# One fused kernel on one core: the order planned with a port shared by VectorE and GpSimd, the softmax sum taken from a column of ones, x kept in float32, and four plain d_ff tiles in place of two

## The chip, the core and the metric

The kernel runs on one core of a Trainium2 chip. The metric is the device time of one execution in microseconds. Five engines matter here: TensorE (PE; PEld is its weight load), VectorE (DVE), ScalarE (ACT), GpSimd (POOL), and SyncE (SP), which issues the DMAs. Each engine works through its own queue in order and waits for the others by semaphores.

## The reference

Three stages follow one another, on 2304 tokens (4 batches of 576) and 512 features.

```python
# 1. attention inside chunks of 64 tokens, 8 heads of 64
scores = q_c @ k_c.T / sqrt(64); scores -= max(scores)
attn = exp(scores); attn /= sum(attn) + 1e-9
x = attn @ v_c                      # (2304, 512) after the heads are put side by side
# 2. gated feed-forward, d_ff = 1536
xn = x / sqrt(mean(x*x) + 1e-6) * rms_g
g = xn @ w_gate; val = xn @ w_val
y = (g * sigmoid(g) * val) @ w_out
# 3. four dense experts of width 1024, weighted by p
p = probs / (sum(probs) + 1e-9)
out = sum_e p[:, e] * (relu(y @ w1[e]) @ w2[e])
```

All inputs and the output are float32, except that the program reads w_gate, w_val and w_out as the 32-bit words of a 64-bit layout and puts the float values together itself.

## The kernel before

**Precision.** A matmul operand in float32 is split into a high part (`xh`, `w[:, 0]`, rounded to fp32r by a copy on ScalarE) and a low part (the rest, a subtraction on VectorE or GpSimd). Each product is three matmuls: high by high, high by low, low by high.

**Attention.** Tokens go in 18 tiles of 128. For a tile, SyncE loads q, k and v (line 380); TensorE transposes q and k (415) and makes the scores (445); VectorE takes the maximum (464) and subtracts it (469); ScalarE takes the exponent (482); VectorE sums the exponents (487), adds 1e-9 (488) and inverts (489); GpSimd multiplies the exponents by the inverse (500; VectorE once); TensorE transposes them (511) and multiplies by v (539); the result is copied out of PSUM (552 or 554) and squared and summed on ScalarE (563); GpSimd takes the root (570, 574); VectorE scales by it and by `rms_g` (580); TensorE transposes the row (591, tile `xtps`); ScalarE writes `xh` (599) and VectorE `xl` (604). Tiles 8 to 17 go in pairs up to the division. PSUM banks for all of this are six buffers of one resource, `a`.

**The gated stage.** Tokens are taken in blocks of 512, 512, 512, 512 and 256, and d_ff in 12 tiles of 128. The first `PLAIN` d_ff tiles (two) are plain products (`proj`, matmuls on line 864, PSUM tiles `gps` and `vps`): 12 matmuls for each d_ff tile, block and matrix. The remaining d_ff tiles go in pairs through a seven-product scheme (`seven_first` and `chain`, line 1021, tile `hps`): for two token blocks and two d_ff tiles it needs seven products of six matmuls where plain work needs eight. The last block of 256 is plain throughout (line 1145). The scheme needs sums of x blocks (`first_operands`): four additions that put `xh + xl` together again (960), four sums (965), four low parts (976), each over 1024 elements a partition, for each of two block pairs. The weights need sums too (`block_weights`: line 774, low parts 800).

**Weights of the gated stage.** `converted` turns 64-bit words into float32: one ScalarE step (652), four on VectorE (656, 660, 664, 668) and an addition (674, VectorE or GpSimd). `weights64` splits a plain tile (692, 698). w_out has 12 such tiles; the products with it are `sum_out` (line 1200, tile `yo`). The gated values are stored to DRAM and loaded again (`hidden`, high part 1165, low part 1169).

**The experts.** Two passes over the experts, the block pair (0, 1) and then (2, 3) with the block of 256: `seven` (line 1021), `plain` (1145), `out_product` (1444, gathered by VectorE on 1467).

**What sets the order.** Nothing is written in order by hand. Class `Plan` (lines 18 to 120) holds a list of steps, each with an engine (or two to choose from), an assumed cost, the steps it needs, the buffers it takes and a rank. It places them one after the other at the earliest time that its own costs give, ranks deciding between equals, and emits them in that order. So every engine's queue has a fixed order, and on the chip only semaphores hold an engine back. Plain products of the gated stage are chained through `last_pe` (line 835), so that they keep the order of the list of units.

## Time and profile before

| | |
|---|---|
| three runs, median | 1285.47 us (1285.41 to 1286.49) |
| the profiled execution | 1285.23 us, of which 1283.4 us lie between its first and its last instruction |
| busy share | PE 98%, PEld 82%, DVE 57%, ACT 39%, POOL 26% |
| busy us | DVE 737.9, ACT 505.7, POOL 336.8 |
| DMA | 101 MB, 79 GB/s over the span, 194 and 195 GB/s in its first two fortieths |

Times are counted from the first instruction of the profiled execution. Matmuls are pipelined, so the busy time of one (0.39 us for 512 columns) is longer than the distance to the next; where the text needs the pace of TensorE it takes the distance from start to start. In rows of the timeline the bracket gives how long the engine stood idle before the instruction, and what released it.

### The profile page before, as it was taken

The numbers are of one execution on the slowest core, as the hardware profiler recorded it, in microseconds if no ns is written. First come the engines' busy times: TensorE is split into PE (matmuls) and PEld (weight loads), VectorE is DVE, ScalarE is ACT, GpSimd is POOL, SyncE is SP. The second block draws the span as 40 slices with busy tenths as digits, with TensorE's granted clock in tenths as the row PEclk, the third lists the DMA queues.
The fourth block names the chain that finished last, engine by engine and source line by source line (L and its number), as shares of the span: only waits on it lengthen the run. The fifth ranks groups of instructions, "written<-read, shape, count | busy, mean of one in ns | idle before, by whom it ended". The sixth has DMA issues, their size and how long they took to land.

```text
span 1283.4 us, 17596 instructions
## 1 busy us (share of the span) xinstructions
PE 1252.3 (98%) x6959; PEld 1051.5 (82%) x6959; DVE 737.9 (57%) x1079; ACT 505.7 (39%) x895; POOL 336.8 (26%) x289
## 2 busy tenths in 40 slices
PE   7989799999999999999999999999999999999998
PEld 6777688888888888988888888878888888888887
DVE  5998985677598262644554445484445344454532
ACT  4767344353454242633333324344233233332320
POOL 2576741132033000221211212143132132231200
PEclk9989999999999999999999999999999999999999
DMA  9862132333266331211211112121111111111102
GB/s 194 195 148 76 54 120 77 113 107 108 82 215 201 126 99 50 76 65 33 66 50 52 48 49 67 50 94 54 34 49 34 33 50 36 48 46 37 34 1 82
DMA packets 118674, 101.05 MB, mean 79 GB/s; under 512 B 62400, under 2 KB 94144, under 8 KB 118592
## 3 DMA queue, kind: packets, MB, share of 16 engines
q1 hardware_dynamic: 118592, 99.93, 25.9%
q8 instruction: 54, 0.88, 0.3%
q14 instruction: 28, 0.23, 0.1%
HBM read 81.04 MB, written 18.87 MB: 78 GB/s over the span
## 4 chain that ended last, share of the span: by engine, by line
PE 66%; DVE 1%; issue 0%; ACT 0%
PE y L1444 30%; PE hps L1021 24%; PE yo L1200 9%; PE hps L1145 4%; DVE acc L1293 0%; DVE xa L1306 0%; DVE acc L1467 0%; ACT xa L1300 0%; DVE w L698 0%; ACT w L692 0%; PE hps L1048 0%; ACT hb L1368 0%
## 5 line engine op out<-in xcount | busy, mean ns | idle before, releaser
L1444 PE MATMUL y<-w,hb 128*128 128x512 f32 x1728 | 400.0, 390 | 1.8 <-DVE acc L1467 1.8
L1444 PEld LDWEIGHTS y<-w,hb 128*128 128x128 f32 x1728 | 324.8, 188 | 70.0 <-DVE acc L1467 2.9
L1021 PE MATMUL hps<-xa,w 128*128 128x512 f32 x1344 | 310.4, 390 | 0.0
L1021 PEld LDWEIGHTS hps<-xa,w 128*128 128x128 f32 x1344 | 251.6, 188 | 53.8 <-DVE p L1055 1.9
L1467 DVE SCALAR_TENSOR_TENSOR acc<-y,pn,acc 128x512 f32<-128x512 f32 x126 | 87.6, 748 | 148.3 <-PE y L1444 148.3
L1035 ACT ACTIVATE hps<-hps 128x512 f32<-128x512 f32 x104 | 60.6, 582 | 241.1 <-PE hps L1021 241.0
L1200 PE MATMUL yo<-ha,w 128*128 128x512 f32 (+1 forms) x720 | 148.4, 368 | 0.1
L1200 PEld LDWEIGHTS yo<-ha,w 128*128 128x128 f32 x720 | 125.5, 189 | 23.1 <-DVE w L698 0.5
L800 POOL TENSOR_TENSOR w<-raw,w 128x512 fp32r<-128x512 f32 (+1 forms) x59 | 80.8, 1380 | 211.4 <-ACT w L792 202.8
L733 POOL TENSOR_TENSOR w<-raw,w 128x512 fp32r<-128x512 f32 x39 | 52.7, 1351 | 236.4 <-ACT w L727 235.7
L792 ACT ACTIVATE w<-raw 128x512 fp32r<-128x512 f32 (+1 forms) x128 | 75.4, 601 | 95.9 <-PE y L1444 59.1
L1021 PE MATMUL hps<-xh,w 128*128 128x512 f32 x320 | 105.9, 391 | 0.5 <-ACT hps L1035 0.4
L1052 DVE TENSOR_TENSOR hps<-hps,p 128x512 f32<-128x512 f32 x52 | 36.3, 698 | 120.8 <-ACT hps L1035 120.8
L1021 PE MATMUL hps<-xs,w 128*128 128x512 f32 x360 | 88.5, 390 | 0.3 <-DVE p L1055 0.3
L774 POOL TENSOR_TENSOR raw<-raw 128x256 f32<-128x256 f32 x46 | 37.0, 805 | 191.4 <-DVE w L800 127.4
L1021 PEld LDWEIGHTS hps<-xs,w 128*128 128x128 f32 x360 | 67.3, 188 | 15.2 <-DVE p L1055 1.3
L1169 DVE TENSOR_TENSOR ha<-sr,ha 128x512 fp32r<-128x512 f32 (+1 forms) x60 | 43.5, 750 | 62.6 <-ACT ha L1165 62.6
L1145 PE MATMUL hps<-xh,w 128*128 128x256 f32 x416 | 76.9, 283 | 0.0
L1372 DVE SCALAR_TENSOR_TENSOR hb<-hps,hb 128x512 fp32r<-128x512 f32 x96 | 65.7, 685 | 16.0 <-ACT hb L1368 14.1
L800 DVE TENSOR_TENSOR w<-raw,w 128x512 fp32r<-128x512 f32 (+1 forms) x69 | 46.3, 672 | 46.5 <-ACT w L792 45.5
L1021 PEld LDWEIGHTS hps<-xh,w 128*128 128x128 f32 x320 | 60.3, 188 | 13.8 <-ACT hps L1035 0.8
L1145 PEld LDWEIGHTS hps<-xh,w 128*128 128x128 f32 x416 | 65.7, 192 | 0.5
(115 smaller groups left out, 1547.3 us busy)
## 6 DMA issues: line engine op xcount, KB each, us to landing
raw<-in_moe_w_dram SPq DMA_DIRECT2D x64, 512.0 KB, 3.5
sr<-sd SPq DMA_DIRECT2D x48, 256.0 KB, 3.1
sd<-s SPq DMA_DIRECT2D x38, 256.0 KB, 2.1
raw<-in_moe_w_gate_dram SPq DMA_DIRECT2D x12, 512.0 KB, 4.2
raw<-in_moe_w_val_dram SPq DMA_DIRECT2D x12, 512.0 KB, 3.6
raw<-in_moe_w_out_dram SPq DMA_DIRECT2D x12, 512.0 KB, 3.6
out_dram<-acc SPq DMA_DIRECT2D x18, 256.0 KB, 2.1
q<-in_q_dram SPq DMA_DIRECT2D x16, 256.0 KB, 4.5
```

The source lines that it names most:

```text
L733: e_.tensor_tensor(out=w[:, 1], in0=part(k), in1=f32(w[:, 0]), op=ALU.subtract)
L774: e_.tensor_tensor(out=block(to), in0=block(one), in1=block(two), op=ALU.subtract)
L792: nc.scalar.activation(out=w1t[key, c][:, ms, 0], in_=a, func=AF.Copy)
L800: e_.tensor_tensor(out=w[:, ms, 1], in0=a, in1=f32(w[:, ms, 0]), op=ALU.subtract)
L1021: nc.tensor.matmul(out=bank[b], lhsT=w[:, m, wi, kk, :], rhs=xx[xi][:, kk, :], start=start and (kk, i) == (0, 0), stop=(kk, i) == (1, 2), ...
L1035: nc.scalar.activation(out=bank[to], in_=bank[frm], func=AF.Copy)
L1145: nc.tensor.matmul(out=got["b"], lhsT=w[:, i, wi, kk, :], rhs=(xh, xl)[xi][REST][:, 2 * m + kk, 0:n], start=(m, kk, k) == (0, 0, 0), stop= ...
L1169: nc.vector.tensor_tensor(out=t[:, i, 1], in0=tiles["sd", j, f], in1=f32(t[:, i, 0]), op=ALU.subtract)
L1200: nc.tensor.matmul(out=y_ps[j, d], lhsT=w[:, wi, d, :], rhs=h[:, hl, :], start=first and p == 0, stop=last and p == 2,)
L1372: nc.vector.scalar_tensor_tensor(out=t[:, i, 1], in0=source(), scalar=0.0, in1=f32(t[:, i, 0]), op0=ALU.max, op1=ALU.subtract)
L1444: nc.tensor.matmul(out=y_ps[j, t], lhsT=h[hl][:, t * P:(t + 1) * P], rhs=w[:, wi].rearrange("p k f -> p (k f)"), start=first and (hl, wi) ...
L1467: nc.vector.scalar_tensor_tensor(out=a, in0=ps, scalar=pc, in1=a, op0=ALU.mult, op1=ALU.add)
```

## The change

- **The planner.** A step can now claim a port. Steps that may run on GpSimd claim it, and VectorE steps that read two SBUF operands or make SBUF-to-SBUF passes are marked so by hand. The planner lets a step with the mark begin only when the last one before it has ended, on either engine. This is a rule for the order alone: no semaphore follows from it.
- **Softmax.** v is loaded into tiles of 66 floats a head, whose last two are set to one at the start. The product with v has 65 columns, the last being the sum of the exponents. The division moves behind the product: VectorE adds 1e-9 to the sums in PSUM, inverts them and multiplies the product on its way out of PSUM. The sum over the exponents, the division on GpSimd and the copy out of PSUM go. The product takes a PSUM tile of two banks (`av`); the resource `a` keeps four.
- **x in float32.** ScalarE copies each transposed tile once more, into `xf`; the sums of `first_operands` read `xf`, and the eight additions of `xh + xl` go.
- **Plain tiles.** `PLAIN` is 4: d_ff tiles 0 and 1 for all five blocks, then 2 and 3 for all five. The steps of a plain product are no longer chained to the other products.
- **Buffers and costs.** The places of the sums, of the weight tiles and some assumed costs change; `STRETCH` goes from 1.6 to 1.3.

```diff
-    def add(self, eng, cost, emit, needs=(), takes=(), rank=0.0, lag=0.0, table=None, after=0.0):
+    def add(self, eng, cost, emit, needs=(), takes=(), rank=0.0, lag=0.0, table=None, after=0.0, port=None):
...
+        n.port = len(n.engs) > 1 and "Pool" in n.engs or eng == "Pool" if port is None else port
...
-        t = max(self.free_at.get(eng, 0.0), n.at)
+        t = max(self.free_at.get(eng, 0.0), n.at, self.port_free if n.port else 0.0)
...
+            if n.port:
+                self.port_free = s + cost
...
-    PLAIN = 2
+    PLAIN = 4
...
-    plan.buffers("a", ["a0", "a1"] + [f"y{d}" for d in range(KD)])
+    plan.buffers("a", [f"y{d}" for d in range(KD)])
+    plan.buffers("av", ["av"])
...
-        plan.buffers("w", [f"x{i}" for i in range(4, NWX)], at)
+        plan.buffers("w", ["x8"], at)
...
-    for j, fs in [(0, [0]), (1, [0]), (0, [1]), (1, [1])] + [(j, range(PLAIN)) for j in range(2, NB)]:
-        for f in fs:
-            units += [("g", ("g", f), j), ("v", ("v", f), j)]
+    for f0 in range(0, PLAIN, 2):
+        for j in range(NB):
+            for f in (f0, f0 + 1):
+                units += [("g", ("g", f), j), ("v", ("v", f), j)]
...
-        def total(_):
-            ee = tiles["ee", key]
-            den = sm_p.tile([P, ng * H, 1], F32, tag="den", name="den")
-            nc.vector.tensor_reduce(out=den, in_=ee, axis=AX.X, op=ALU.add)
-            nc.vector.tensor_scalar(out=den, in0=den, scalar1=1e-9, scalar2=None, op0=ALU.add)
-            nc.vector.reciprocal(out=den, in_=den)
...
-            dv = add({"Pool": 1.1, "DVE": 0.69} if i < 2 else "Pool", 1.1, divide, needs=[tot], rank=rank(i, 11))
...
-            s3 = add("PE", 0.436, transpose_e, needs=[dv] + s3s, takes=["a", "eT"], rank=rank(i, 10))
+            s3 = add("PE", 0.436, transpose_e, needs=[ex] + s3s, takes=["a", "eT"], rank=rank(i, 10))
...
-                ps = a_bank(tag, [P, H, D], "xps")
+                ps = ps_a.tile([P, 2, 512], F32, tag=tag, name="xps")
+                ps = ps[:, :, 0:HP * VW].rearrange("p b (h e) -> p b h e", e=VW)
...
+            def total(_, i=i):
+                den = sm_p.tile([P, 2, HP, 1], F32, tag="den", name="den")
+                ps = tiles["xps", i]
+                nc.vector.tensor_scalar(out=den, in0=ps[:, :, :, D:D + 1], scalar1=1e-9, scalar2=None, op0=ALU.add)
+                nc.vector.reciprocal(out=den, in_=den)
+                tiles["den", i] = den
...
+                nc.vector.tensor_tensor(
+                    out=xs.rearrange("p (b h d) -> p b h d", b=2, h=HP), in0=tiles.pop(("xps", i))[:, :, :, 0:D],
+                    in1=tiles.pop(("den", i)).to_broadcast([P, 2, HP, D]), op=ALU.mult,
+                )
...
-            cx = add({"ACT": 0.6, "DVE": 0.69}, 0, copy_x, needs=[s4], rank=rank(i, 7))
-            cx.gives.append(("a", s4, 0))
+            tot = add("DVE", 0.4, total, needs=[s4], rank=rank(i, 7.5))
+            cx = add("DVE", 0.66, divide, needs=[tot], rank=rank(i, 7))
+            cx.gives.append(("av", s4, 0))
...
-            sl = add("DVE", 0.9, scale, needs=[ro, g_node], rank=rank(i, 4))
+            sl = add("DVE", 0.7, scale, needs=[ro, g_node], rank=rank(i, 4), port=True)
...
+            def keep(_, i=i):
+                j, t = tile_block[i]
+                if j not in xf:
+                    xf[j] = big.tile([P, KD, blocks[j][1]], F32, tag=f"acc{j}", name="xf")
+                nc.scalar.activation(out=xf[j][:, :, t * P:(t + 1) * P], in_=tiles["xtps", i], func=AF.Copy)
...
-        for fn, cost in ((c2, 0.5), (c3, 0.88), (c6, 0.5), (c7, 0.75)):
-            n = add("DVE", cost, fn, needs=[n], rank=rank)
-        n = add({"DVE": 0.83, "Pool": 1.45}, 0, c8, needs=[n], rank=rank)
+        for fn, cost in ((c2, 0.43), (c3, 0.69), (c6, 0.43), (c7, 0.69)):
+            n = add("DVE", cost, fn, needs=[n], rank=rank, port=True)
+        n = add({"DVE": 0.69, "Pool": 1.4}, 0, c8, needs=[n], rank=rank)
...
-            node = pe(cost, emit, [w_node[key], *x_nodes[j]] if kk == 0 else [], ["h"] if kk == 0 else [], due[u])
+            node = add("PE", cost, emit, needs=[node] if kk else [w_node[key], *x_nodes[j]],
+                       takes=[] if kk else ["h"], rank=due[u])
...
-        t1 = whole("A21")
-        t2 = whole("A22")
-        s1 = sum_of("A22", "A21", "A22", ALU.add, t1, t2)
...
+        s1 = sum_of("S1", "A21", "A22", ALU.add, *needs)
+        s3 = sum_of("S3", "A11", "A21", ALU.subtract, s1)
+        s2 = sum_of("S2", "S1", "A11", ALU.subtract, s3)
...
+        for i in range(3):
+            t = v_tiles[f"v_{i}"] = at_p.tile([P, H, VW], F32, tag=f"v_{i}", name="v")
+            nc.gpsimd.memset(t[:, :, D:VW], 1.0)
```

Three places show what this does to the queues. First VectorE in the middle of the attention, around a scaling by the root (580 before, 584 now). Before:

```order
L580 SCALAR_TENSOR_TENSOR xs<-xs,rinv,g_bc 128x512
L660 SCALAR_TENSOR_TENSOR f64a<-f64a,raw 128x4x128
L487 TENSOR_REDUCE den<-e 128x16
L488 TENSOR_SCALAR den<-den 128x16
L489 RECIPROCAL den<-den 128x16
L464 TENSOR_REDUCE mx<-sc 128x8
L604 TENSOR_TENSOR xl_99<-xtps,xh_94 128x4x128
```

Now, from the first instruction of the first weight tile (673) on:

```order
L673 TENSOR_SCALAR raw<-f64a 128x512
L548 TENSOR_SCALAR den<-xps 128x8
L549 RECIPROCAL den<-den 128x8
L554 TENSOR_TENSOR xs<-xps,den 128x512
L677 SCALAR_TENSOR_TENSOR f64a<-f64a,raw 128x4x128
L681 TENSOR_SCALAR raw<-f64a 128x512
L685 SCALAR_TENSOR_TENSOR raw<-raw 128x512
L584 SCALAR_TENSOR_TENSOR xs<-xs,rinv,g_bc 128x512
L691 TENSOR_TENSOR f64a<-f64a,raw 128x4x128
```

The sum over the exponents (487) is gone from VectorE, and the inverse stands directly ahead of the division out of PSUM (554), for one tile at a time. The first weight tile (673 here, 656 before) stands behind seven scalings now, and behind three before.

Second TensorE where the plain products of the last block end; `xh_93` is the high part of x of block 0, `xh_97` that of block 4. Before, the seven products begin (1048, 1021):

```order
L864 MATMUL vps<-xl_102,w 128x256
L864 MATMUL vps<-xh_97,w 128x256
L1048 MATMUL hps<-xh_93,w 128x512 x2
L1021 MATMUL hps<-xh_93,w 128x512
L1021 MATMUL hps<-xl_98,w 128x512
```

Now the plain products of d_ff tiles 2 and 3 begin, again with block 0:

```order
L880 MATMUL vps<-xl_102,w 128x256
L880 MATMUL vps<-xh_97,w 128x256
L880 MATMUL gps<-xh_93,w 128x512
L880 MATMUL gps<-xl_98,w 128x512
L880 MATMUL gps<-xh_93,w 128x512 x2
```

A second round of plain products for all blocks stands between the last transposed tile of x and the first seven products.

Third VectorE in the conversion of w_out. Before (656 to 668 convert, 1169 is the low part of a gated tile, 698 that of a weight tile):

```order
L656 TENSOR_SCALAR raw<-f64a 128x512
L660 SCALAR_TENSOR_TENSOR f64a<-f64a,raw 128x4x128
L664 TENSOR_SCALAR raw<-f64a 128x512
L668 SCALAR_TENSOR_TENSOR raw<-raw 128x512
L1169 TENSOR_TENSOR ha<-sr,ha 128x512 x2
L698 TENSOR_TENSOR w<-f64a,w 128x512
```

Now (673 to 685 convert, 691 is the addition, 1180 and 715 the low parts):

```order
L673 TENSOR_SCALAR raw<-f64a 128x512
L677 SCALAR_TENSOR_TENSOR f64a<-f64a,raw 128x4x128
L715 TENSOR_TENSOR w<-f64a,w 128x512
L681 TENSOR_SCALAR raw<-f64a 128x512
L685 SCALAR_TENSOR_TENSOR raw<-raw 128x512
L1180 TENSOR_TENSOR ha<-sr,ha 128x512
L691 TENSOR_TENSOR f64a<-f64a,raw 128x4x128
```

The addition (691) and more of the low parts (715) stand on VectorE now. Over the twelve tiles of w_out VectorE has 8 additions and 10 low parts of weights where it had 3 and 5; GpSimd has 4 and 2 where it had 9 and 7.

## Rows read from the trace of the kernel before

**Rows 1.** The page's first line.

```profile
span 1283.4 us, 17596 instructions
```

**Rows 2.** Busy us by stretch: PE, PEld, DVE, ACT, POOL (instructions), PE clock, DMA share, GB/s.

```profile
0.00:37.10 37.10, 30.18 (x493) 27.03 (x495) 22.67 (x43) 19.62 (x38) 8.59 (x18) 0.95 0.95 199
37.10:135.80 98.70, 88.44 (x1118) 73.36 (x1112) 94.58 (x128) 66.53 (x115) 69.16 (x62) 0.97 0.55 130
135.80:160.30 24.50, 17.25 (x95) 15.42 (x96) 23.63 (x22) 7.13 (x12) 18.68 (x9) 0.89 0.14 46
160.30:345.80 185.50, 185.09 (x903) 156.50 (x903) 125.03 (x188) 81.86 (x145) 46.47 (x41) 1.00 0.31 102
345.80:413.60 67.80, 67.30 (x317) 55.54 (x315) 64.10 (x89) 32.72 (x58) 23.40 (x16) 1.00 0.57 187
```

**Rows 3.** Chain of waits, in order of time: start, length, engine, tile, line, count.

```profile
412.88 0.70 DVE w L698
...
562.45 9.52 PE hps L1021 x42
571.97 10.88 PE y L1444 x48
...
863.33 5.75 PE hps L1145 x48
```

**Rows 4.** Timeline of TensorE: start, length, engine, line, operation, count, idle before.

```profile
4.86 0.60 PE L415 MATMUL tps<-ident,q 128*128 128x128 f32 x4
...
24.18 1.15 PE L445 MATMUL sc<-kT,qT 64*64 64x64 f32 x32
25.25 0.66 PE L415 MATMUL tps<-ident,q 128*128 128x128 f32 x4
25.75 0.60 PE L415 MATMUL tps<-ident,k 128*128 128x128 f32 x4
26.18 0.60 PE L591 MATMUL xtps<-ident,xs 128*128 128x128 f32 x4
...
55.22 0.47 PE L864 MATMUL gps<-xh,w 128*128 128x512 f32 x1
...
135.98 0.63 PE L591 MATMUL xtps<-ident,xs 128*128 128x128 f32 x4 [1.00 <-DVE xs L580]
...
160.27 1.05 PE L1048 MATMUL hps<-xh,w 128*128 128x512 f32 x2
```

**Rows 5.** Timeline of VectorE.

```profile
35.65 0.20 DVE L489 RECIPROCAL den<-den 128x8 f32<-128x8 f32 x1
...
37.12 0.42 DVE L656 TENSOR_SCALAR raw<-f64a 128x512 int32<-128x512 int32 x1
37.58 0.69 DVE L660 SCALAR_TENSOR_TENSOR f64a<-f64a,raw 128x512 int32<-128x512 int32 x1
...
45.05 0.68 DVE L554 COPY xs<-xps 128x512 f32<-128x512 f32 x1
45.65 0.67 DVE L604 TENSOR_TENSOR xl<-xtps,xh 128x512 fp32r<-128x512 f32 x1
...
70.22 2.07 DVE L660 SCALAR_TENSOR_TENSOR f64a<-f64a,raw 128x512 int32<-128x512 int32 x1
...
134.67 1.17 DVE L580 SCALAR_TENSOR_TENSOR xs<-xs,rinv,g_bc 128x512 f32<-128x512 f32 x1
```

**Rows 6.** Timeline of GpSimd.

```profile
69.38 2.36 POOL L960 TENSOR_TENSOR xw<-xh,xl 128x1024 f32<-128x1024 f32 x1
```

**Rows 7.** Groups on GpSimd, 37.1 to 135.8 us: count, busy us, mean ns, idle before.

```profile
L965 POOL TENSOR_TENSOR xw<-xw 128x1024 f32<-128x1024 f32 x4 | 10.5, 2619 | 0.2
L574 POOL TENSOR_TENSOR rinv<-ms,half_neg 128x1 f32<-128x1 f32 x15 | 10.3, 685 | 1.2
L570 POOL TENSOR_SCALAR ms<-ms 128x1 f32<-128x1 f32 x15 | 5.1, 337 | 7.0 <-ACT junk L563 6.2
L698 POOL TENSOR_TENSOR w<-f64a,w 128x512 fp32r<-128x512 f32 x2 | 2.7, 1351 | 1.2 <-ACT w L692 1.2
```

More of the change, by code (lines that the diff above doesn't have):

```diff
@@ L99, in run @@
                 i = owner.ids[k]
-                if i in self.lent and n.end > self.lent_until:
-                    r = self.lent[i]
                 if callable(r):
@@ L391, in tile_attention_moe_moe2 @@
     x_nodes = {j: [] for j in range(NB)}
+    f_nodes = {j: [] for j in range(NB)}
+    xf = {}
     groups = [[i] for i in range(PAIR_FROM)] + [[i, i + 1] for i in range(PAIR_FROM, NTILE, 2)]
@@ L713, in tail @@
         stage["tail"] = at
-        plan.res["xc"] += [x for x in plan.res["w"] if x[1] == "x5"]
-        plan.res["w"] = [x for x in plan.res["w"] if x[1] != "x5"]
+        plan.res["w"] = [x for x in plan.res["w"] if ":" not in x[1]]
     def weights(keys, src):
@@ L891, in silu_of, with times_of @@
         sil_node[j, f] = (c, own or c)
[L893 removed]
+    def times_of(j, f, source, needs, rank, frees, port=False):
         n = blocks[j][1]
@@ L899, in product @@
             nc.vector.tensor_tensor(out=s, in0=s, in1=source(), op=ALU.mult)
-        c = add("DVE", 0.15 + n * 0.00106, product, needs=[*needs, s_n], rank=rank)
+        c = add("DVE", 0.15 + n * 0.00106, product, needs=[*needs, s_n], rank=rank, port=port)
         c.gives.append(frees)
@@ L945, in home, with src @@
                     t[m] = [y[:, 0], y[:, 1]]
-                else:
-                    i = {"S2": 0, "S3": 2}[m]
-                    t[m] = [opened()["w"].tile([P, 2, n], F32R, tag=f"x{i + k}", name="xs1") for k in range(2)]
             return t[m]
-        tmp = {}
+        def src(m):
+            j, k = PLACE[m]
+            return xf[j][:, k:k + 2, :]
         def eng_of(e):
             return nc.gpsimd if e == "Pool" else nc.vector
-        def whole(m):
-            def emit(eng, tag):
-                tmp[m] = pool_of(tag).tile([P, 2, n], F32, tag=tag, name="xw")
-                a, b = piece(m)
-                eng_of(eng).tensor_tensor(out=tmp[m], in0=f32(a), in1=f32(b), op=ALU.add)
-            return add(wide, 0, emit, needs=needs, takes=["w"], rank=rank + 0.1 * next(seq))
@@ L963, in sum_of @@
         def sum_of(to, one, two, op, *n_):
             def emit(eng):
-                eng_of(eng).tensor_tensor(out=tmp[to], in0=tmp[one], in1=tmp[two], op=op)
+                eng_of(eng).tensor_tensor(out=src(to), in0=src(one), in1=src(two), op=op)
             return add(wide, 0, emit, needs=[*n_], rank=rank + 0.1 * next(seq))
-        nodes = {m: needs[-1] for m in ("A11", "A12", "A22")}
-        def parts(m, src, *n_):
+        nodes = {"A11": x_nodes[ja][-1], "A12": x_nodes[ja][-1], "A22": x_nodes[jb][-1]}
@@ L971, in high, with parts @@
+        def parts(m, *n_):
             def high(_):
-                nc.scalar.activation(out=home(m)[0], in_=tmp[src], func=AF.Copy)
+                nc.scalar.activation(out=home(m)[0], in_=src(m), func=AF.Copy)
             def low(eng):
                 h, l = home(m)
-                eng_of(eng).tensor_tensor(out=l, in0=tmp[src], in1=f32(h), op=ALU.subtract)
-            h = add("ACT", 1.05, high, needs=[*n_], rank=rank + 0.1 * next(seq))
+                eng_of(eng).tensor_tensor(out=l, in0=src(m), in1=f32(h), op=ALU.subtract)
+            h = add("ACT", 1.05, high, needs=[*n_, *held], rank=rank + 0.1 * next(seq))
@@ L1000, in tile_attention_moe_moe2 @@
+        l3 = parts("S3", s3)
+        l2 = parts("S2", s2)
+        l1 = parts("S1", s2, *plain_done[jb])
+        s4 = sum_of("S4", "A12", "S2", ALU.subtract, s2)
+        l4 = parts("S4", s4)
+        done = add("none", 0.0, lambda _: None, needs=[l1, l2, l3, l4], rank=rank)
+        if p:
+            done.then = lambda at: plan.buffers("w", [f"acc{j}:{i}" for j in PAIRS[1] for i in range(2)], at)
+        x1[p] = {"home": home, "nodes": nodes, "done": done}
     PARTS = ((0, 0), (0, 1), (1, 0))
@@ L1109, in seven_first, with done @@
             if p == 0:
-                pr_["P3"].then = lambda at: plan.buffers("hh", ["xh0", "xl0", "xh1", "xl1"], at)
+                def done(at):
+                    plan.buffers("hh", ["xh0", "xl0", "xh1", "xl1"], at)
+                    plan.buffers("xc", [f"x{i}" for i in range(4)], at)
+                    plan.buffers("w", ["x4", "x5"], at)
+                pr_["P3"].then = done
             else:
@@ L1113, in done @@
                     plan.buffers("hp", ["xh2", "xl2", "xh3", "xl3"], at)
-                    plan.buffers("xc", [f"x{i}" for i in range(4)], at)
+                    plan.buffers("xc", ["x7"], at)
+                    plan.buffers("w", ["x6"], at)
                 pr_["P3"].then = done
@@ L1175, in hidden @@
         hi = add("ACT", act, high, needs=[ld], rank=rank - 2)
-        lo = add("DVE", dve, low, needs=[hi], rank=rank - 2)
+        lo = add("DVE", dve, low, needs=[hi], rank=rank - 2, port=True)
         in_flight.append(lo)
@@ L1318, in parts @@
                 x_taken[m] = h
-            nodes[m] = add("DVE", 1.18, low(m), needs=[h], rank=rank + 0.1 * next(r))
+            nodes[m] = add("DVE", 1.21, low(m), needs=[h], rank=rank + 0.1 * next(r), port=True)
             return nodes[m]
         def s(m, one, two, op, *n_):
-            return add("DVE", 1.18, sum_of(m, one, two, op), needs=[*needs, *n_], rank=rank + 0.1 * next(r))
+            return add("DVE", 1.21, sum_of(m, one, two, op), needs=[*needs, *n_], rank=rank + 0.1 * next(r), port=True)
         l11 = parts("A11")
```

122 lines of the change are left out of this document (56 added, 66 removed).

## The prediction

> **What bounds the kernel now.** The profiled execution took 1285.23 us, its span is 1283.4 [rows 1]; the 1.8 us between them stay. The sum is made against 1285.23, which lies 0.2 us under the median of the three runs (1285.47).
>
> I read the stretches first, to see where TensorE stands idle. From 160.3 to 345.8 it is busy for 185.09 of 185.50 us, and from 345.8 to 413.6 for 67.30 of 67.80; before 160.3 it is not, and VectorE is: 94.58 of 98.70 us between 37.1 and 135.8 [rows 2]. Busy time flatters TensorE, so I count its work by the pace it has where nothing holds it. The chain of waits gives 9.52 us for 42 matmuls of 512 columns and 10.88 for 48, both 0.2267 us each, and 5.75 for 48 of 256 columns, 0.120 each [rows 3]. The timeline gives four transpositions in 26.18 - 25.75 = 0.43 us and the scores of a tile in 25.25 - 24.18 = 1.07 [rows 4]. I take the product with v like the scores.
>
> Ahead of the first seven products stand 72 groups of four transpositions (31.0), 36 groups of scores and products with v (38.5), 192 matmuls of 512 columns (43.5) and 48 of 256 (5.8): 118.8 us. From the first transposition at 4.86 that would end at 123.7; the seven products begin at 160.27 [rows 4]. TensorE has lost 36.6 us there. What held it is VectorE: the last transposition of x waits for its scaling, which ends at 135.84, and starts at 135.98 [rows 4, 5].
>
> **The change part by part.** *Plain tiles.* Two d_ff tiles leave the scheme. It needed 2 matrices x 2 block pairs x 42 = 168 matmuls for them, plain work needs 192: 24 x 0.2267 = 5.4 us more, all on TensorE. The 256-column work is the same. In exchange the work ahead of the first seven products grows by 192 and 48 matmuls, to 168.1 us, and what depends on VectorE last moves forward: behind the last transposition of x the new queue has 276 matmuls of 512 and 96 of 256 columns, 62.6 + 11.5 + 0.4 = 74.5 us, so 93.6 lie ahead of it and it could start at 98.5 if nothing waited. With L for what TensorE loses up to the first seven products,
>
> time = 1285.2 + 5.4 - 36.6 + L = 1254.0 + L, and L = (start of that transposition) - 98.5 + 0.5.
>
> The 0.5 is for small waits behind it. VectorE needs 41.6 us of its own (instructions between that scaling and the first use of the seven-product sums, at the durations below) for the sums and weights of the seven products, and has 74.5 for it; that is what hides them now, and if the cover were short the excess would be L.
>
> *When VectorE reaches the first weight tile.* It began it at 37.12 [rows 5]. Ahead of it stood 43 instructions, 21.6 us at the durations below; now 70, 36.7 us. The difference of 15.5 (first loads, waits for TensorE) kept, that is 52.2. The loads agree: ahead of this weight tile SyncE's queue now holds 13 tiles each of q and k, nine of v, the gain and the weight, 10.0 MB, which takes 50 us at the 199 GB/s of the first stretch, in which the DMA engines are 95% busy [rows 2]. I take 52.
>
> *From there to the last scaling.* Unhindered durations from start to start: 0.62 us for a pass of 512 elements (45.65 - 45.05 = 0.60, and a little for dependence), 0.66 with three operands or two in SBUF, 0.44 for the one-operand passes of the conversion (37.58 - 37.12 = 0.46), 0.2 for the small ones [rows 5]. Before: 59 passes at 0.62, 27 at 0.66, 13 at 0.44, nine longer ones (9.8 us in all) and 18 small: 73.4 us, against 98.7 on the clock. The missing 25.3 us are mostly VectorE waiting inside its instructions: one that takes 0.69 at 37.58 takes 2.07 at 70.22, while GpSimd is in an instruction from 69.38 to 71.74 [rows 5, 6]. GpSimd was busy for 69.16 us in the stretch [rows 2]: 0.37 us lost for each us of it. Now VectorE has 46 passes at 0.62, 22 at 0.66, 12 at 0.44 and 24 small: 52.8 us; the sums over the exponents are gone, the divisions stand for the copies. GpSimd has lost the divisions and the additions of the two parts of x; 10 roots of 0.337 + 0.685, six weight steps of 1.35 and four sums of 2.62 are left in the stretch, 28.8 us [rows 7]. At 0.37 that is 10.7 us. The last transposition then starts at 52 + 52.8 + 10.7 = 115.5.
>
> Two prices the trace does not show. The addition of 1e-9 reads eight sums out of PSUM: between 0.2 like the inverse and 0.6 like a full pass; I take 0.2, its size decides, and 0.6 would add 4 us. The loss per us of GpSimd lies between 0 and 1: the order is now made to keep the two apart, but nothing on the chip does; I keep the measured 0.37. At 0 TensorE's own work is the limit (first rival).
>
> *Beside other work, at nothing.* 16 copies into float32 on ScalarE, which is idle for 32.2 of the 98.7 us [rows 2]; the 65th column (1.6% of 19 us); the ones, written before the first product. Between the two passes of the experts VectorE and ScalarE have the same queue as before, so the loss there stays.
>
> *w_out.* From 345.8 to 413.6, VectorE is busy for 64.10 of 67.80 us and its low part at 412.88 stands in the chain of waits [rows 2, 3]. By the durations above it had 50.1 us of work, now 56.3, ten more instructions; GpSimd's come down from 16 to six. The overhead of 17.7 us scaled by 6/16 is 6.6: 62.9 us, under the 65.6 that TensorE needs there (a seventh product, three schemes, the small block, 11 steps of 2.72). Counted at nothing; if the overhead stays, it is 74.0 and costs 6.2.
>
> Sum: L = 115.5 - 98.5 + 0.5 = 17.5, time = 1271.5 us, 1.1% less.
>
> **The rivals.** *TensorE itself.* If VectorE and GpSimd do not meet, the last transposition is set by TensorE's work behind the first plain product. That product starts six us behind the first weight step, at 58 (one conversion, a copy, a low part), and 47 us of queue lie between: 105. L = 7, 1261 us. For it: GpSimd's work in the stretch falls from 69.16 to 28.8 us; against it: VectorE's queue alone ends at 104.8, so both engines would have to run without a gap.
>
> *They meet every time: the order does not do what it is made for.* Then each of the 28.8 us of GpSimd is lost on VectorE: the start is 133.6, L = 35.6, 1289.6 us, slower. It decides from a start of about 130, that is 0.87 us lost per us. Against it: now only 0.37 is, since half of VectorE's instructions read PSUM. The Trainium skill, SBUF — State Buffer, Who interferes with whom, has the lock behind this: a VectorE instruction with two inputs in SBUF and a GpSimd instruction that reads SBUF exclude each other for the whole length of whichever came first. By that rule the order alone decides, and an order that drifts from its plan gives back what it won; the row at 70.22 agrees, ending 0.55 us behind GpSimd's.
>
> *Banks.* The product with v holds two PSUM banks, and six buffers for the rest become four, each now held for one ScalarE copy longer. If TensorE waits for banks so that the last transposition stays at 136, nothing is won and the 24 matmuls are paid: L = 38, 1292 us, slower; above 130 it decides too. Against it: 94.58 of 98.70 say that VectorE, not banks, sets the pace.
>
> *Loads.* If a tile of v in rows of 66 floats takes twice as long to load, nine tiles of 0.26 MB at 199 GB/s put the first weight 12 us later: L = 29.5, 1283.5 us. The Trainium skill, DMA: Bandwidth & Descriptors, How a descriptor splits into AXI transactions, says that a transfer that does not start at a multiple of 256 bytes costs one transaction more; a head's 256 bytes now start every 264. No run here shows such a load.
>
> *w_out on VectorE*, as worked out: 1271.5 + 6.2 = 1277.7 us.
>
> **How the numbers follow.** Forecast 0.54, TensorE itself 0.16, w_out 0.11, loads 0.06, meeting every time 0.05, banks 0.08. The forecast's own range is 1264 to 1278 (0.1 to 0.6 lost per us, and 0.6 for the small sum). The range 1258 to 1284 takes in all but the two slower rivals, with 3 us below the fast one for the loss at a lower granted clock (0.89 in the stretch of the idle gap [rows 2]), part of which may go too. 0.2% is about what can be told from no change: 2.6 us. Faster 0.84; same 0.06, half of the loads and the near edges of the slower two; slower 0.10.
>
> **What would show it.** In the new profile: first plain product near 58, the last transposition of x near 115, the first seven products some 75 us behind it with no wait at their start, near 190. VectorE's conversion instructions at 0.69 with fewer of 1.5 and more; GpSimd's busy time to the last scaling under half. The prediction is wrong if the last transposition comes at 130 or later, if TensorE has gaps between it and the seven products, or if a gap of several us appears in the first 12 steps with w_out.

## The result, and the profile after

The changed kernel took 1269.26 us (1268.70 to 1270.13, four runs), the kernel before 1285.56 in the same comparison: a ratio of 0.9872 (95% 0.9855 to 0.9889), 1.3% less. 1271.5 was forecast. The profiled execution took 1268.7 us.

The head of its page, against [rows 1] and the small table:

```profile
span 1266.7 us, 17516 instructions
...
PE 1252.4 (99%) x6983; PEld 1053.8 (83%) x6983; DVE 709.2 (56%) x1141; ACT 492.8 (39%) x878; POOL 204.9 (16%) x196
```

The stretches, cut where the same things happen as in [rows 2]: the first weight tile, the last scaling, the first seven products, w_out.

```profile
0.00:54.30 54.30, 49.26 (x862) 43.22 (x864) 37.81 (x70) 34.90 (x68) 6.79 (x26) 1.00 0.88 202
54.30:114.40 60.10, 56.66 (x701) 47.40 (x698) 53.09 (x105) 40.98 (x74) 25.97 (x30) 0.97 0.54 137
114.40:190.60 76.20, 76.08 (x383) 64.59 (x382) 52.97 (x67) 26.40 (x43) 22.87 (x11) 1.00 0.29 98
190.60:329.00 138.40, 138.40 (x680) 117.54 (x679) 85.26 (x147) 59.80 (x108) 25.46 (x19) 1.00 0.29 98
329.00:397.00 68.00, 68.00 (x324) 57.26 (x324) 61.22 (x101) 34.26 (x61) 8.14 (x6) 1.00 0.59 194
```

The stretch from the first weight tile to the last scaling is 60.1 us long instead of 98.7, and GpSimd is busy for 25.97 us of it instead of 69.16. Behind it TensorE is idle for 0.12 us in all up to 190.6, at the full granted clock (1.00); the gap in which it was busy for 17.25 of 24.5 us, at 0.89, is gone.

TensorE's timeline, against [rows 4]: first plain product, last transposition of x, first seven products of the gated stage, first seven products of the experts.

```profile
61.09 0.48 PE L880 MATMUL gps<-xh,w 128*128 128x512 f32 x1
...
115.66 0.60 PE L595 MATMUL xtps<-ident,xs 128*128 128x128 f32 x4
...
190.64 0.63 PE L1054 MATMUL hps<-xh,w 128*128 128x512 f32 x2
...
514.85 0.63 PE L1054 MATMUL hps<-xa,w 128*128 128x512 f32 x2
```

None of them has waited. The last transposition does not wait for its scaling either: that ended at 114.34 (113.59 + 0.75, in the rows below), and TensorE was in plain products until 115.66. It had been busy with hardly a break for 42 us by then:

```profile
73.60:115.66 42.06, 41.77 (x484) 34.55 (x483) 35.31 (x71) 27.11 (x50) 19.01 (x25) 1.00 0.36 96
```

VectorE's timeline, against [rows 5]: a conversion and its neighbours, the last scaling, and what comes behind it.

```profile
54.32 0.42 DVE L673 TENSOR_SCALAR raw<-f64a 128x512 int32<-128x512 int32 x1
54.65 0.16 DVE L548 TENSOR_SCALAR den<-xps 128x8 f32<-128x8 f32 x1
...
62.03 0.69 DVE L677 SCALAR_TENSOR_TENSOR f64a<-f64a,raw 128x512 int32<-128x512 int32 x1
...
113.59 0.75 DVE L584 SCALAR_TENSOR_TENSOR xs<-xs,rinv,g_bc 128x512 f32<-128x512 f32 x1
115.58 0.69 DVE L608 TENSOR_TENSOR xl<-xtps,xh 128x512 fp32r<-128x512 f32 x1 [1.24 <-ACT xf L616]
...
121.30 2.62 DVE L673 TENSOR_SCALAR raw<-f64a 128x512 int32<-128x512 int32 x1
123.96 2.77 DVE L677 SCALAR_TENSOR_TENSOR f64a<-f64a,raw 128x512 int32<-128x512 int32 x1
```

Up to the last scaling conversions take 0.42 and 0.69, as in [rows 5] where nothing holds them. Behind it they take 2.6 to 2.9, because GpSimd now does its long work there:

```profile
115.62 5.21 POOL L975 TENSOR_TENSOR xf<-xf 128x1024 f32<-128x1024 f32 x2 [2.62 <-ACT xf L616]
120.79 5.39 POOL L986 TENSOR_TENSOR xs<-xf,xs 128x1024 fp32r<-128x1024 f32 x2
```

That costs nothing, since TensorE has plain products of the second round until 190.6.

### The profile page after: what moved, and what is told of

It reads as the page before. It is cut to its first block, busy times and chain, and to the rows that moved or that the text cites. A ratio compares the mean times of both kernels' runs of the same rounds, so it can differ in the third digit from the quotient of the medians.

```text
span 1266.7 us, 17516 instructions
## 1 busy us (share of the span) xinstructions
PE 1252.4 (99%) x6983; PEld 1053.8 (83%) x6983; DVE 709.2 (56%) x1141; ACT 492.8 (39%) x878; POOL 204.9 (16%) x196
## 4 chain that ended last, share of the span: by engine, by line
PE 95%; DVE 3%; issue 1%; ACT 1%; DMA 0%; SPq 0%; POOL 0%; POOLq 0%; ACTq 0%
PE hps L1027 36%; PE y L1455 30%; PE yo L1211 12%; PE hps L1156 5%; PE vps L880 4%; PE gps L880 3%; PE xps L536 1%; PE sc L461 1%; PE tps L431 1%; PE xtps L595 1%; PE eps L507 1%; DVE acc L1304 0%; DVE f64a L677 0%; DMA v<-in_v_dram 0%; PE warm L1508 0%
## 5 line engine op out<-in xcount | busy, mean ns | idle before, releaser
L816 DVE TENSOR_TENSOR w<-raw,w 128x512 fp32r<-128x512 f32 (+1 forms) x98 | 62.1, 648 | 48.2 <-ACT w L808 47.5
L749 POOL TENSOR_TENSOR w<-raw,w 128x512 fp32r<-128x512 f32 x30 | 39.8, 1326 | 268.5 <-ACT w L743 268.5
L1383 DVE SCALAR_TENSOR_TENSOR hb<-hps,hb 128x512 fp32r<-128x512 f32 x96 | 65.8, 685 | 17.2 <-ACT hb L1379 15.2
L1180 DVE TENSOR_TENSOR ha<-sr,ha 128x512 fp32r<-128x512 f32 (+1 forms) x60 | 38.0, 656 | 65.5 <-ACT ha L1176 65.5
L816 POOL TENSOR_TENSOR w<-raw,w 128x512 fp32r<-128x512 f32 (+1 forms) x30 | 40.3, 1345 | 203.0 <-ACT w L808 203.0
L1156 PE MATMUL hps<-xh,w 128*128 128x256 f32 x352 | 65.2, 283 | 0.0
L1379 ACT ACTIVATE hb<-hps 128x512 fp32r<-128x512 f32 x96 | 56.9, 592 | 18.4 <-PE hps L1027 17.8
L1027 PE MATMUL hps<-xh,w 128*128 128x512 f32 x176 | 58.7, 389 | 0.0
L1156 PEld LDWEIGHTS hps<-xh,w 128*128 128x128 f32 x352 | 55.7, 192 | 0.4
L1417 ACT ACTIVATE hb<-hps 128x256 fp32r<-128x256 f32 x32 | 12.3, 383 | 103.6 <-PE hps L1156 103.6
L1176 ACT ACTIVATE ha<-sr 128x512 fp32r<-128x512 f32 (+1 forms) x60 | 32.8, 579 | 48.9 <-PE yo L1211 41.7
```

Of the source, the lines that this page charges most:

```text
L749: e_.tensor_tensor(out=w[:, 1], in0=part(k), in1=f32(w[:, 0]), op=ALU.subtract)
L816: e_.tensor_tensor(out=w[:, ms, 1], in0=a, in1=f32(w[:, ms, 0]), op=ALU.subtract)
L1027: nc.tensor.matmul(out=bank[b], lhsT=w[:, m, wi, kk, :], rhs=xx[xi][:, kk, :], start=start and (kk, i) == (0, 0), stop=(kk, i) == (1, 2), ...
L1156: nc.tensor.matmul(out=got["b"], lhsT=w[:, i, wi, kk, :], rhs=(xh, xl)[xi][REST][:, 2 * m + kk, 0:n], start=(m, kk, k) == (0, 0, 0), stop= ...
L1379: nc.scalar.activation(out=t[:, i, 0], in_=source(), func=AF.Relu)
L1383: nc.vector.scalar_tensor_tensor(out=t[:, i, 1], in0=source(), scalar=0.0, in1=f32(t[:, i, 0]), op0=ALU.max, op1=ALU.subtract)
```

## The experiments

"Old" and "off" below mean one part of the change undone in the changed kernel. All ratios are to the kernel before, whose median was 1286.5 us in each of the three comparisons that these runs come from. L is TensorE's lost time up to the first seven products, as in the prediction: their start, less 4.9 for the first transposition and 168.1 of work (118.8 with two plain tiles). Where the text says that TensorE lost time "by its pace", it is the time from start to start, less what the matmuls between need at the prediction's paces.

**Order for the port off.**

```diff
-        n.port = len(n.engs) > 1 and "Pool" in n.engs or eng == "Pool" if port is None else port
+        n.port = False
```

> The changed kernel, with every step's port claim off: the planner orders as if VectorE and GpSimd never met; all other edits stay. VectorE's work up to the last scaling is almost the same (92.7 us at unhindered durations against 91.1), GpSimd gets 264 instructions in all instead of 201. Theory A (the order keeps the two engines apart, and that is most of the gain): about 32 us of GpSimd lie between the first weight tile and the last scaling (10 roots, three additions, five low parts, four sums); at 0.37 us lost per us, as in the kernel before, the last transposition of x moves from 115.7 to about 126 and the time to 1277 to 1282 us. Theory B (GpSimd has so little left there that the order matters little): last transposition at 115 to 119, time 1268 to 1272 us.

Measured: 1275.11 us, ratio 0.9907 (0.9891 to 0.9924), 5.9 us over the changed kernel by the medians and 4.5 by the ratios; last transposition at 122.02, seven products at 195.94. The time lies between the two theories, nearer A. By its pace TensorE lost 5.3 us more up to the seven products and 3.2 more between them and the experts'. VectorE, GpSimd and TensorE around 82 us show what happens:

```profile
81.80 2.25 DVE L691 TENSOR_TENSOR f64a<-f64a,raw 128x512 f32<-128x512 f32 x1
83.98 0.68 DVE L918 TENSOR_TENSOR s<-s,vps 128x512 f32<-128x512 f32 x1
84.57 2.23 DVE L584 SCALAR_TENSOR_TENSOR xs<-xs,rinv,g_bc 128x512 f32<-128x512 f32 x1
```

```profile
80.93 5.33 POOL L975 TENSOR_TENSOR xf<-xf 128x1024 f32<-128x1024 f32 x2
```

```profile
86.95 0.63 PE L595 MATMUL xtps<-ident,xs 128*128 128x128 f32 x4 [4.22 <-DVE xs L584]
```

An addition and a scaling, each reading two operands from SBUF, end just after one of GpSimd's two sums each; the product between them, with one operand in PSUM, keeps its 0.68. TensorE then waits 4.22 us for the scaling. The order keeps such meetings rare. The run does not separate this from the load, since without the claims GpSimd also gets more to do: 33.0 us in the stretch instead of 26.0.

**Two plain tiles.**

```diff
-    PLAIN = 4
+    PLAIN = 2
```

> The changed kernel with two plain d_ff tiles instead of four. Theory A (the second round of plain products covers the sums and weights of the seven products): the last transposition of x stays near 116, TensorE has only 25.7 us of plain work behind it (141.3 - 115.7 in the changed kernel's timeline), VectorE needs 41.6 us and more, so the seven products begin or wait until 157 to 165; two tiles more in the scheme cost 43.8 us behind it: 1268.7 - 190.6 + 43.8 + (157 to 165) = 1279 to 1287 us. Theory B (the cover is not needed; the gain is all in the attention): they begin near 141.5 and the 24 matmuls are saved: 1263 us.

Measured: 1270.31 us, 0.9867 (0.9845 to 0.9889): not to be told from the changed kernel. Both theories missed. The seven products began at 142.25, so nothing held them at their start; then they waited:

```profile
156.91 1.01 PE L1027 MATMUL hps<-xs,w 128*128 128x512 f32 x2 [2.56 <-ACT w L808]
158.46 4.63 PE L1027 MATMUL hps<-xs,w 128*128 128x512 f32 x10 [0.53 <-DVE w L816]
```

By its pace TensorE lost 6.7 us between 150 and 165. About half of it was standing still; the rest was a granted clock of 0.50, the lower level, behind the first wait, at which matmuls were about 0.44 us apart instead of 0.227:

```profile
157.19:164.01 6.82, 6.29 (x15) 4.41 (x15) 5.44 (x11) 1.73 (x4) 0.00 (x0) 0.50 0.24 77
```

The 6.7 us are little more than what the 24 matmuls cost (5.4): within the scatter the second round pays for itself and no more.

**Old softmax.** The sum over the exponents, the division on GpSimd and the copy out of PSUM come back (v stays in rows of 66):

```diff
+        tot = add("DVE", 0.5 + 0.58 * ng, total, needs=[ex], ...)
+            dv = add({"Pool": 1.1, "DVE": 0.69} if i < 2 else "Pool", 1.1, divide, needs=[tot], ...)
-                    in1=tiles.pop(("den", i)).to_broadcast([P, 2, HP, D]), op=ALU.mult,
```

> The changed kernel with the old softmax: sum over the exponents on VectorE ahead of the transposition, division on GpSimd (17 of 18 tiles), a copy out of PSUM by either engine, a product with v of 64 columns into one bank; v still lies in rows of 66 floats. Theory A (the part matters because it takes work from both engines): VectorE has 98.1 us up to the last scaling instead of 91.1, GpSimd 12 or so divisions of 1.1 us in the stretch; kept apart by the order they hold VectorE up by something between 0 and 13 us: last transposition at 122 to 134, time 1275 to 1287 us. Theory B (VectorE's 7 us of waiting in that stretch take the extra work in): 116 to 118, time 1268 to 1271 us.

Measured: 1270.31 us, 0.9873 (0.9852 to 0.9893). The time is B's, the place is A's: the last transposition came at 129.29, 13.6 us later, but the planner had put 39 more of the plain matmuls ahead of it, and the seven products began at 195.03, 4.4 later, in the slowest of these runs (1273.1).

**No copy of x.** The eight additions of `xh + xl` write the buffers that ScalarE filled:

```diff
-            if tile_block[i][0] != REST:
+            if False:
                 kp = add("ACT", 0.6, keep, needs=[s5], rank=rank(i, 0))
...
+                eng_of(eng).tensor_tensor(out=src(m), in0=a, in1=b, op=ALU.add)
```

> The changed kernel without the float32 copy of x on ScalarE: eight additions of the two parts of x, 1024 elements a partition each, come back on VectorE or GpSimd and write the same buffers. VectorE has 95.2 us up to the last scaling instead of 91.1. Theory A (the stretch up to the last transposition is VectorE's): it moves by 4 us and what three GpSimd additions of 2.6 us cost at 0.37 (3 us) to about 120 to 123, time 1272 to 1276 us. Theory B (the additions are hidden behind the second plain round, which has 74.5 us for 41.6 us of VectorE's work): last transposition within 2 us of 115.7 and the time within 2.5 us of the changed kernel's.

Measured: 1266.07 us, 0.9837 (0.9817 to 0.9856): 3.2 us under the changed kernel by the medians, which neither theory said. The last transpositions stand at 124.18, yet the seven products at 187.88, 2.8 earlier than in the changed kernel. What TensorE waited for, first in the changed kernel, then here:

```profile
PE xtps L595 <- ACT qT L440: 2.7, 2, 2.1
```

```profile
PE xtps L595 <- ACT qT L440: 0.3, 1, 0.3
```

The wait of 2.1 in the changed kernel, and the stretch right behind it:

```profile
69.46 0.66 PE L595 MATMUL xtps<-ident,xs 128*128 128x128 f32 x4 [2.12 <-ACT qT L440]
...
70.12:73.53 3.41, 3.41 (x38) 3.20 (x39) 2.38 (x6) 2.09 (x4) 2.22 (x1) 0.50 0.89 239
```

Idle for 2.12 us, TensorE then ran 3.41 us at a granted clock of 0.50. Without the copy it has neither, and the clock stays at 1.00 up to the seven products.

Run again beside the changed kernel:

> The changed kernel as it is, once more, on the same chip as the three kernels run with it, so that differences of two or three us between them can be read without going through different chips. Both theories: 1268.5 to 1270.5 us.

> The changed kernel without the float32 copy of x, as in the run that took 1266.1 us, beside the changed kernel. Theory A (the 16 copies on ScalarE stand ahead of copies that TensorE waits for, and the eight additions that they replace lay under plain products): 2 to 4 us under the changed kernel of the same runs, seven products again 2 to 3 us earlier, no wait of 2 us for the copy of a transposed q near 69 us. Theory B (the difference came from the chip): within 1.3 us of it.

The changed kernel took 1268.39 us, 0.9860 (0.9846 to 0.9874); without the copy 1266.50, 0.9851 (0.9833 to 0.9868), seven products at 186.77 against 191.08. That is 1.9 us, just short of theory A's two, with the seven products 4.3 earlier instead of 2 to 3. The wait near 69 and the lower clock behind it are there again with the copy and absent without. The intervals overlap, so two us are likely and not certain. What holds in both pairs is that the copy brings nothing. Of the versions run, the one without it has the lowest median.

**The second round alone**, in the kernel before (two plain tiles to four, the changed kernel's list of units, and its name for buffers that nobody takes again):

```diff
-    PLAIN = 2
+    PLAIN = 4
```

> The kernel before with four plain d_ff tiles in two rounds over all blocks (0 and 1, then 2 and 3), and nothing else of the change. TensorE's queue has 67.3 us of plain work behind the last transposition of x, instead of 15.3. Behind the first seven products the changed kernel needs 1076 us. Theory A (cover is worth what the gaps from 150 to 168 us cost before, 8.4 + 1.4 us, against 5.4 us of more matmuls): last transposition still at 130 to 136, seven products at 198 to 204, time 1276 to 1282 us. Theory B (VectorE, hindered by GpSimd, sets the pace and the plain round brings nothing of its own): 1286 to 1291 us, the 24 matmuls on top. If the second round alone were the change's gain: 1270 us.

Measured: 1313.26 us, 1.0213 (1.0199 to 1.0227), far outside both theories. The seven products began at 207.79 (L = 34.8, before 36.6), so nothing was lost up to there. By its pace TensorE lost 28.5 us between there and the experts: 11.1 up to 225 and 16.3 between 380 and 450, in w_out, part of it at the lower clock level. The longest waits there:

```profile
PE yo L1201 <- ACT w L693: 6.0, 6, 1.8
...
PE hps L1022 <- ACT w L793: 4.5, 1, 4.5
...
PE yo L1201 <- POOL w L699: 2.6, 3, 0.9
```

Four plain tiles alone, then, run into waits for weights that the changed kernel does not have. Which of its other parts takes them away, the buffers for weights or the order of the conversions, was not tried.

**The order alone**, in the kernel before: the port rule, the claims on scaling and conversions, and their assumed costs.

```diff
+        t = max(..., self.port_free if n.port else 0.0)
+            sl = add("DVE", 0.7, scale, ..., port=True)
```

> The kernel before with the planner's port rule, the claims on the scaling and the conversions, and the changed kernel's assumed costs for them; softmax, sums and two plain tiles as before. VectorE has 104.3 us up to the last scaling at unhindered durations (96.1 in the kernel before, which lost 25 more inside its instructions), GpSimd loses some steps to it. Theory A (the order alone takes the loss away, also with GpSimd's full load): conversions at 0.69, last transposition at 126 to 130, seven products from 143 on with stalls of 3 to 8 us, time 1268 to 1276 us. Theory B (the order helps only because the other edits took work off GpSimd; with 69 us of it the two engines stand in each other's way whatever the order): last transposition at 134 or later, time 1282 to 1290 us.

Measured: 1280.37 us (1276.18 to 1282.16), 0.9956 (0.9942 to 0.9970): 6 us of some 16, between the theories. Last transposition at 140.08, later than before although VectorE lost half as much inside its instructions (table below): it had 11 more of them in the stretch and waited 10.7 us there, mostly for TensorE, instead of 3.0. Seven products at 153.79, 6.5 us earlier, in the fastest of these runs.

**More GpSimd work that the order does not know of.**

```diff
+                if i >= 7:
+                    for _ in range(2):
+                        nc.gpsimd.tensor_tensor(out=dump, in0=g_bc[:, 0:256], in1=g_bc[:, 256:512], op=ALU.add)
```

> The changed kernel, with two additions of 256 elements a partition on GpSimd (both inputs in SBUF, a result that nobody reads) behind each root of tiles 7 to 17: 22 instructions, about 15 us by half of the 1.33 us that its additions of 512 take. The queues of the other engines are word for word those of the changed kernel. Theory A (VectorE loses 0.37 us for each us of GpSimd that the order does not know of): scalings and conversions longer, last transposition at 120 to 122, time 1274 to 1276 us. Whole exclusion: 15 us, 1284 us. Theory B (VectorE has 7 us of waits there, or the two do not meet): within 2 us of the changed kernel.

Measured: 1271.15 us, 0.9881 (0.9867 to 0.9894); last transposition at 118.66.

```profile
L583 POOL TENSOR_TENSOR dump<-g_bc 128x256 bf16<-128x256 f32 x22 | 18.1, 825 | 0.9
```

VectorE lost 5.5 us more inside its instructions (table below), 0.31 per us of GpSimd. The listed waits of VectorE shrank from 5.7 to 3.8 us, so only 3.0 reached the transposition. One of these 3.0 was there already at the first weight tile (55.29). A had the rate, B the effect.

**Two parts at once.** No copy and two plain tiles; old softmax and two plain tiles; old softmax and order off (the diffs above, joined).

> The changed kernel without the float32 copy of x (the eight additions are back) and with two plain d_ff tiles. Without the copy alone the time was 1266.1 us, with two plain tiles alone 1270.3 (5.4 us of matmuls less, 6 us of waits at the start of the seven products). TensorE has 17.3 us of plain work behind the last transposition, which comes at 124 or so; seven products from 142. Theory A (the additions stand ahead of the sums, and nothing covers them now): waits at the start of the seven products grow from 6 to 10 us or more, 1268 to 1276 us. Theory B (they come early enough; the parts add): 1266.1 + 1.0 = 1267 us or less, down to 1262.

> The changed kernel with both the old softmax and two plain d_ff tiles; each alone cost 1.0 us. VectorE has 98.2 us up to the last scaling, and TensorE 14.6 us of plain work behind the last transposition instead of 74.1. Theory A (the two stand in for each other: with the old softmax the last transposition came 13.6 us later, and only the second plain round kept that from the end): last transposition near 130, seven products from 144 with waits of 6 to 12 us for their weights, 1275 to 1281 us. Theory B (the parts add): 1271 us.

> The changed kernel with the old softmax and with the port claims off; alone they cost 1.0 and 5.9 us. Theory A (order and softmax are two answers to the same meeting of VectorE and GpSimd: the order matters more where GpSimd has more to do): 10 divisions of 1.1 us more in the stretch that the order does not keep apart; at 0.19 to 0.37 us lost per us, 2 to 4 us more than the sum: 1278 to 1282 us. Theory B (the parts add): 1276 us.

The first took 1268.66 us, 0.9865 (0.9852 to 0.9879): seven products already at 137.75, but 11.4 us lost between 140 and 165 by TensorE's pace, where two plain tiles alone lost 6.7. That is theory A by its waits, at the edge of its time: the additions do lean on the second round, though the time alone does not tell the theories apart. The second took 1272.84, 0.9894 (0.9881 to 0.9908): between adding up and standing in. The third took 1282.39, 0.9966 (0.9953 to 0.9978), where adding up gives 1276: theory A. Order and softmax in one table (the changed kernel was compared twice):

| ratio to before | new softmax | old softmax |
|---|---|---|
| order for the port | 0.9872, 0.9860 | 0.9873 |
| order off | 0.9907 | 0.9966 |

By the ratios the order is worth 4.5 to 6 us with the new softmax and 12 with the old; the softmax is worth 7.6 us without the order, and with it at most 1.7, within the scatter. The parts overlap: both answer the same meeting of VectorE and GpSimd. The scaling by the root, 18 times in each kernel, shows it most plainly: its mean is 1121 ns before, 757 in the changed kernel, 956 with the order off, and 1050 with both off.

```profile
L580 DVE SCALAR_TENSOR_TENSOR xs<-xs,rinv,g_bc 128x512 f32<-128x512 f32 x18 | 20.0, 1121 | 0.0
```

```profile
L584 DVE SCALAR_TENSOR_TENSOR xs<-xs,rinv,g_bc 128x512 f32<-128x512 f32 x18 | 13.5, 757 | 0.0
```

```profile
L584 DVE SCALAR_TENSOR_TENSOR xs<-xs,rinv,g_bc 128x512 f32<-128x512 f32 x18 | 17.2, 956 | 0.0
```

```profile
L596 DVE SCALAR_TENSOR_TENSOR xs<-xs,rinv,g_bc 128x512 f32<-128x512 f32 x18 | 18.7, 1050 | 0.7 <-POOL rinv L590 0.7
```

With both off 4 us of gain are left for the remaining parts together (four plain tiles with the new buffers, the copy, the free placing). They were not taken apart further; chaining the plain products again moves only nine plain matmuls in TensorE's queue from behind the last transposition to ahead of it, and was not tried.

## Why the prediction was right, step by step

*The bound and the formula.* L came out at 17.6 (190.64 - 173.0), forecast 17.5. Where TensorE does not wait behind the last transposition, the seven products start there plus the plain work behind it. But the last transposition is a fixed point only for one order. Without the copy it stands over 8 us later and L is 14.9, because more plain work stood ahead of it. L is TensorE's lost time, wherever the planner puts the transposition. By its pace TensorE lost, in us:

| | to the first plain product | from there to the last transposition | to the first seven products | to those of the experts |
|---|---|---|---|---|
| before | 12.8 | 15.2 | 8.6 | 3.2 |
| changed | 9.8 | 7.3 | 0.5 | 0.1 |
| order off | 10.2 | 12.6 | 0.1 | 3.3 |
| two plain tiles | 11.0 | 7.3 | 0.1 | 6.8 |
| no copy of x | 9.8 | 4.9 | 0.1 | 0.4 |
| before, four plain tiles | 12.5 | 20.6 | 1.7 | 28.5 |

The change takes away 22.2 us of such losses and adds 5.4 us of matmuls, which leaves 16.8; the profiled executions differ by 16.5. The prediction laid all of the 36.6 us up to the seven products at the last transposition's wait for VectorE. 8.6 of them came behind it, nearly all in one wait of the kernel before for another instruction of VectorE, the gating of a plain tile:

```profile
157.54 0.58 PE L864 MATMUL vps<-xh,w 128*128 128x256 f32 x1 [7.07 <-DVE s L899]
```

*The 2.8 us too many.* From the first seven products to those of the experts the kernel before took 531.49 - 160.27 = 371.2 us (the first time from its timeline, the second in [rows 4]), the changed one 324.2. Two tiles less in the scheme explain 43.8; 3.2 us more went. The term of 36.6 us ended at 160.27, but the kernel before went on losing behind it:

```profile
161.12 0.63 PE L1021 MATMUL hps<-xh,w 128*128 128x512 f32 x1
161.55 0.46 PE L1021 MATMUL hps<-xl,w 128*128 128x512 f32 x1
...
167.42 0.50 PE L1021 MATMUL hps<-xh,w 128*128 128x512 f32 x1 [0.41 <-ACT hps L1035]
```

The first matmuls, from the row at 160.27 on, are 0.43 apart instead of 0.227, at the lower clock level; with the wait at 167.42 that is 1.4 us; 1.0 more went around 380, 0.4 at 413, and the rest in pieces of about 0.1. The term was mis-sized by these 3.2 us.

*First weight tile.* Forecast at 52, came at 54.32; first plain product 58, came at 61.09. The queue ahead was longer than its VectorE work and the loads say.

*From there to the last scaling.* 63.5 us forecast, 60.0 taken, for two reasons that pull apart. The loss to GpSimd was put at 10.7, by 0.37 us per us. Measured as VectorE's durations less the shortest of the same operation and shape in any of these runs, added up over the stretch from the first weight tile to the last scaling:

| | lost by VectorE, us | GpSimd busy, us | per us |
|---|---|---|---|
| before | 26.7 | 69.3 | 0.39 |
| before, four plain tiles | 25.4 | 61.1 | 0.42 |
| order off | 13.3 | 33.0 | 0.40 |
| order off, old softmax | 18.1 | 48.5 | 0.37 |
| no copy of x | 10.6 | 35.7 | 0.30 |
| before, with the order | 13.9 | 51.9 | 0.27 |
| old softmax | 10.3 | 42.4 | 0.24 |
| changed, more GpSimd | 9.9 | 43.5 | 0.23 |
| changed | 4.4 | 26.0 | 0.17 |

0.37 to 0.42 is the rate of an order that does not know of the port, in four kernels; in the five whose order does (one of them with extra work that it does not know of), it is 0.17 to 0.30. Against these 6 us stand 5.7 us in which VectorE waited for TensorE and ScalarE, which the forecast had left out (52.8 + 4.4 + 5.7 is 62.9, so the unhindered durations were a little high as well, and the forecast's own counts add up to 53.1, not 52.8).

*What set the last transposition.* The forecast let it start where VectorE ends. VectorE ended at 114.34, and TensorE came to it 1.3 us later, out of its own queue. From 73.6 on TensorE lost only 2.7 us by its pace, while VectorE waited 3.4 us for TensorE. So the end of this stretch was the first rival's: 47.2 us of TensorE's queue behind the first plain product. It came at 115.66 and not at 105 because that product started at 61.09 instead of 58 and 7.3 us were lost behind it, 4.7 of them up to 73.6, with the wait at 69.46 and the lower clock. The extra GpSimd work agrees: it cost VectorE 5.5 us, and TensorE's queue 2.0. That 115.5 was hit with the wrong engine at the end, and with a late first tile against a shorter stretch, is largely luck; what the prediction had right is that the loss to GpSimd falls and that the queue behind the transposition runs without a wait.

*The addition out of PSUM.* 0.16 us against 0.2.

*ScalarE's copies at nothing.* Wrong: without them the kernel was no slower, and 2 to 3 us faster by the medians. 41 of 60 us busy does not mean that a copy is free. TensorE's loss is at the wait of 69.46 and the lower clock behind it. How the copies bring that about is not shown: ScalarE had worked without a break since 58.86 when it came to that q, on only one of the copies (60.44) but on two loads of its function tables (63.58 and 66.05, 1.28 us each). Without the copies one such load stands there, because the planner's order changed too.

*The second round as cover for 41.6 us of VectorE's work.* Too high: with one round TensorE lost 6.7 us there, not 16 or more. The sums of the first pair do not wait for the last transposition.

*w_out.* VectorE 62.9 us forecast, 61.22 measured in the stretch of 68.0, in which TensorE did not wait. In the kernel before with four plain tiles it did, and lost 16.3 us there by its pace.

*The other rivals.* TensorE itself did become the bound, from 73.6 us on, as said above. The engines did not meet every time: VectorE lost 4.4 us beside 26.0 of GpSimd. Banks: no wait of TensorE for a bank above 0.3 us. Loads: a tile of v needs 4.2 us from issue to landing, 4.8 before:

```profile
v<-in_v_dram SPq DMA_DIRECT2D x16, 256.0 KB, 4.2
```

The tiles of q and k, whose rows did not change, came down as well, from 4.5 and 4.7 to 3.7 and 3.9, so the load around them was lighter; the rival's doubling did not come. A small cost of the rows of 66 floats is not ruled out. By the Trainium skill (DMA: Bandwidth & Descriptors, How a descriptor splits into AXI transactions) 256 bytes that start off a multiple of 256 take one transaction more; the 4.2 us do not show it.

## What to carry to other kernels

Two engines that hinder each other can be helped by taking work off one or by ordering the two; try both before adding the gains, as each can take a large part of what the other would bring (here 6 us or more of 12, and about 6 of 7.6). Measure the loss per us of the second engine once in the old order and do not assume it for a new one. Cover behind a bottleneck is worth only the wait that it covers: one run with the cover removed tells whether it pays for its own work. A forecast that hits its marker has not shown which engine set it: look whether the marker waited, and for whom.

## What the runs showed of the hardware

A pass with a single SBUF input was held as long as one with two: the conversion at 121.30 took 2.62 us instead of 0.42 beside GpSimd's sums, while a product with one operand in PSUM kept 0.68 beside them (at 83.98, with the order off). The Trainium skill (SBUF — State Buffer, Who interferes with whom) says both, the first for tensor_scalar in a mode that uses both ports; the trace agrees, though in which mode this conversion ran is not shown. So it is not semaphores alone that hold an engine back.

GpSimd instructions in a row gave VectorE one instruction between each two of them: five VectorE instructions of 1.73 to 2.88 us ran between 119.65 and 132.0, in step with GpSimd's. By the durations that they take elsewhere (0.42 to 0.69) VectorE lost some 9.7 of these 12.4 us, against 0.17 to 0.42 us per us of GpSimd from the first weight tile to the last scaling.
